# The end of a two-layer transformer kernel laid out anew: value products first, reciprocals on query rows, and one queue for last block, partials and leftovers

## The chip, the cores and the metric

The kernel runs on one core of a Trainium2 chip. Its engines work side by side, each through its own queue in order: TensorE (PE) multiplies matrices into the accumulation memory PSUM, VectorE (DVE) and ScalarE (ACT) do elementwise work, GpSimd (POOL) a few small things, SyncE (SP) issues transfers. The metric is device time in microseconds (us), the median of several runs; a profiled execution of the same program gives the trace that is read here.

## The reference

Two kinds of layer alternate over 2048 rows of 512 numbers. Softmax attention with 32 query heads of width 16 shares one key and one value head; a feed-forward layer of width 1792 uses ReLU. Each has a layer norm ahead of it and a residual around it.

```python
def _A_ref(x, wq, wk, wv, wo):
    q = (x @ wq).reshape(B, S, H, Dh).transpose(0, 2, 1, 3)
    k = x @ wk
    v = x @ wv
    p = softmax(einsum("bhqd,bkd->bhqk", q, k) * Dh ** -0.5)
    o = einsum("bhqk,bkd->bhqd", p, v)
    return o.transpose(0, 2, 1, 3).reshape(B, S, H * Dh) @ wo

def _B_ref(x, w1, w2):
    return relu(x @ w1) @ w2

x = x + _A_ref(_layernorm(x), A_wq, A_wk, A_wv, A_wo)
x = x + _B_ref(_layernorm(x), B_w1, B_w2)
x = x + _A_ref(_layernorm(x), A_wq, A_wk, A_wv, A_wo)
x = x + _B_ref(_layernorm(x), B_w1, B_w2)
```

## The kernel before

The program is fully unrolled. A plain and slower version of it (`exact`, tag x) stands behind a check of the inputs' range and does not run here; all names in the trace begin with f, the fast version's tag.

**Units and steps.** The rows are cut into four blocks of 512 queries. A unit U is four heads of one block, so each layer has 32 units, and each unit has 16 steps, one for each 128 keys. A step is two score products into the PSUM tiles st0 and st1 (each 128 x 2 x 512 numbers, two banks of 2 KB a partition), an exponential on ACT for each into the tile p, and a value product on PE into the pair acc and acc2. The value rows carry a column of ones, so that the accumulators hold the unnormalised outputs and the softmax's sums side by side. Score and value products use 64x32 pieces of the array, 8 matmuls for a pass of 512 columns. A step can be *cut*: DVE splits p into two halves of 16 bits, and the value product takes 24 short matmuls instead of 8 in f32.

**Chains.** When a block's attention is done, a generator `chain(L, b)` issues all the rest of it in pieces, each a `yield`: the output projection with wo (row tiles s = 0 to 3 of 128 rows), the residual's *gain* (`added`, a DVE operation that reads PSUM and adds to xt), the norm's statistics (`stats`: two DVE operations, then two on POOL) and its `apply`, the transposition back into xt, then for pairs of 128 hidden columns `up` (ReLU on ACT into hh, the low part hl on DVE, both reading PSUM) and, for four of them at a time, `down` with a second gain. In f16 each product is three matmuls, high by high, high by low and low by high.

**The planner.** `timed` lays out the steps by a model of the engines' clocks (`_Account`): whenever PE is free it looks ahead over three choices, a score, a value product or a piece of leftover work from the chains, and takes the first move of the best sequence. What it chooses is PE's order for good. While steps run, leftover work goes through 64x32 pieces in two PSUM tiles named misc (`batch`), with a small read by DVE (`seen`) between its two turns. When no steps are left the kernel is *solo*: a job is then twelve (or six) full 128x128 matmuls, `mm3`, into the next of two misc tiles, read by ACT and DVE. A chain's generator says "lag" when its next piece isn't ready by the planner's account.

**The end, `closing`.** The last two units, 62 and 63, do not go through memory as the others do but stay on the chip (`ends`). The old order is: the 9 *partials* of row tile 0 (the output projection's three finished quarters, `out_early`), `joined`, the other 27 partials, the first weights of the last block (`fetch`), then a loop that gives PE to the last block's chain whenever the planner's account says it is ready, and else to the leftovers of the block before. `joined` multiplies each end with two matrices of zeros and ones (`make_joins`), in f32: one picks the outputs, one spreads each head's sum over its 16 rows. DVE takes 512 reciprocals a partition of the spread sums, then multiplies, and ACT and DVE split the rows into high (ot2[0]) and low (ot2[1]). Three *finals* for each row tile complete the output projection. The partials and finals of row tiles 0 and 1 are accumulated in the two halves of st0, those of 2 and 3 in the two halves of st1. The last chain transposes its normed rows through acc and acc2 and goes on to `up` and `down` in solo form. `bounded`, `least` and `flag` check ranges, between its first pieces.

The planner's account compares exact regions of a tile. The order of PE against the readers of PSUM on the chip is made by the compiler's framework, from the program's order and the tiles that are read and written.

Of the kernel before, what the change touches and what calls it, by code (L numbers as in the profile page):

```python
# [9 lines left out]
F32 = mybir.dt.float32  # L10
# [4 lines left out]
AF = mybir.ActivationFunctionType  # L15
ALU = mybir.AluOpType
AX = mybir.AxisListType.X
MAX, MUL, SUB, ADD = ALU.max, ALU.mult, ALU.subtract, ALU.add

P = 128  # L20
S = 2048
D = 512
# [202 lines left out]
class _Net:  # L225
# [54 lines left out]

    def misc(self):
        return self.pp.tile([P, D], F32, name=self.tag + "misc", bufs=3 if self.exact else 2)
# [721 lines left out]
    def out_early(self, s):  # L1004

        if s % 2 == 0:
            self.bank = self.pp.tile([P, 2, D], F32, name=f"{self.tag}st{s // 2}")
        ps = self.bank[:, s % 2]
        ops = [o for G in range(3) for o in self.out_parts(s, G)]
        for i, (a, b) in enumerate(ops):  # L1010
            self.nc.tensor.matmul(ps, a, b, start=(i == 0), stop=False)
        self.early = (self.early or []) + [ps]

    def joined(self):

        nc, V = self.nc, self.nc.vector
        l, o = (self.pp.tile([P, D], F32, name=self.tag + n) for n in ("acc", "acc2"))
        for k, ps in ((1, l), (0, o)):
            for u in range(2):
                nc.tensor.matmul(ps, self.joins[:, k, u], self.ends[u], start=(u == 0), stop=(u == 1))  # L1020
        r = self.ends_inverse = self.wt("rinv", [P, D])
        t = self.wt("oraw", [P, D])
        h, low = self.ot2[0][:, 3], self.ot2[1][:, 3]
        for c in (slice(0, 256), slice(256, D)):
            V.reciprocal(r[:, c], l[:, c])
            V.tensor_mul(t[:, c], o[:, c], r[:, c])
            nc.scalar.activation(h[:, c], t[:, c], AF.Copy)
            V.tensor_sub(low[:, c], t[:, c], h[:, c])

    def bounded(self):  # L1030

        r, t = self.ends_inverse, self.wt("oraw", [P, D])
        m = self.wt("kmx", [P, 4], bufs=1)
        self.nc.vector.tensor_scalar(t, r, 1.0 / LMAX, None, op0=ALU.is_ge)
        self.nc.vector.scalar_tensor_tensor(t, r, 1.0 / LMIN, t, op0=ALU.is_le, op1=MUL)
        self.nc.vector.tensor_reduce(m[:, 0:1], t, axis=AX, op=ALU.min)
        self.nc.vector.tensor_mul(self.good[:, 0:1], self.good[:, 0:1], m[:, 0:1])

    def make_joins(self):

        self.joins = self.wq2[0].bitcast(F32).rearrange("p c (u m) -> p (c u) m", u=2)[:, 0:4].rearrange(
            "p (k u) m -> p k u m", k=2)
        self.nc.gpsimd.memset(self.joins.rearrange("p k u m -> p (k u m)"), 0.0)
        v = self.ident.rearrange("p (j t d) -> p j t d", t=2, d=DH)
        for u in range(2):
            for k, src in enumerate((v[:, :, 0], v[:, :, 1, 0:1].to_broadcast([P, 4, DH]))):
                dst = self.joins[:, k, u, 64 * u:64 * u + 64].rearrange("p (j d) -> p j d", d=DH)
                self.nc.gpsimd.tensor_copy(dst, src)

    def closing(self, chain):  # L1050

        self.out_early(0)
        self.joined()
        for s in range(1, 4):
            self.out_early(s)
        self.fetch(1, NB - 1)
        old, self.gens = self.gens, []
        chain()
        main, free, outs = self.gens, 0.0, self.outs
        while old:  # L1060
            turn = main if self.outs == outs and self.now >= free else old
            self.gens, self.solo = turn, turn is main
            w = self.advance()
            if turn is main:
                free = self.free if isinstance(w, tuple) else 0.0
        self.gens, self.solo = main, True
# [3 lines left out]
    def chain(self, L, b):  # L1070
# [38 lines left out]
        if self.early:  # L1109
            for s in range(4):  # L1110
                ps, parts = self.early[s], self.out_parts(s, 3)
                yield from self.soon([x for o in parts for x in o])
                for i, (x, y) in enumerate(parts):
                    nc.tensor.matmul(ps, x, y, start=False, stop=(i == 2))
                    yield 1.0
                added(s, ps)
                todo.append(self.stats(xs[s]))
                ready(s)
                if s:
                    todo[s - 1] = self.apply(*todo[s - 1])  # L1120
                if s > 1:
                    yield from self.transposed(todo[s - 2], s - 2, bank="acc2" if s > 2 else "acc")
            todo[3] = self.apply(*todo[3])
            for s in (2, 3):
                yield from self.transposed(todo[s], s, bank="acc2" if s > 2 else "acc")
# [411 lines left out]
    def timed(self, steps, operands, ready, front, back, product, after, cut):  # L1537
# [66 lines left out]
        while len(done) < n:  # L1604
            k, j, due = state[5:8]
            cut_some()
            if chance and self.now >= chance[0][0] - LATE:
                e1, e, i = chance.pop()
                if (self.asked and self.gens and due >= 3.0 and not pend and i > j and self.coming > NEAR
# [18 lines left out]
            kind = choose(state)  # L1628
            rate = self.rate(step, due) if self.gens else 0.0
# [272 lines left out]
```

## Time and profile before

| what | value |
|---|---|
| runs shown | 2226.67 us median of 3 (2226.18 to 2227.86) |
| profiled execution, its own time | 2224.62 us |
| its span from first to last instruction | 2222.7 us, mean clock of PE 0.994 |
| last exponential issued | 2105.40 us from the span's start |
| first up-projection of the last block | 2142.68 us |
| last output transfers issued from | 2212.57 us |

All times inside the trace count from the start of the span. A row of the timeline gives start, duration, engine, operation, output and input tile, shape, count, and in brackets how long the engine was idle before it and what released it. All instructions show line L193, the helper through which the planner records them, so the tile names tell them apart: p and acc are the steps, fmisc leftovers and solo jobs, fst scores and the last output projection, ot the attention rows, xt residual rows and transposed rows. Rows with "| busy, mean ns | idle" are groups. Rows that begin with a stretch of time give for each of PE, PEld (weight loads), DVE, ACT and POOL the busy time and count, then the granted clock of PE (1.00 is full), the share of transfers and GB/s. A matmul's shown end includes its way through the array, so in a run of full-size matmuls the starts lie 0.2157 us apart while each lasts 0.38.

### The profile page before, as it was taken

To read this page: it belongs to the slowest core of one execution; us is meant where nothing else is said; L and a number is where in the kernel's file an instruction comes from. 1 tells how busy PE (TensorE), PEld (TensorE's weight loads), DVE (VectorE), ACT (ScalarE), POOL (GpSimd) and SP (SyncE) were. 2 spreads that over 40 slices of the span, in tenths; PEclk is the share of its full clock that TensorE was granted. 3 is DMA by queue.
4 is the path that set the end of the run, shared out by engine and by line. 5 is a ranking of instruction groups with operands and counts; after the bars stand their busy time and mean duration, and the time that the engine had idled before them with its cause. 6 is when DMAs were issued, how large, how long until landed. Compare 5 with 4: busy or idle time off the path is not lost.

```text
span 2222.7 us, 127244 instructions
## 1 busy us (share of the span) xinstructions
PE 2147.8 (97%) x59873; PEld 1255.0 (56%) x59873; DVE 1207.4 (54%) x1944; ACT 1980.6 (89%) x2112; POOL 280.3 (13%) x320
## 2 busy tenths in 40 slices
PE   7999999999999999999999999999999999999988
PEld 3444446665667555555546855557555556565533
DVE  6526535544565555655575666565635545544552
ACT  6999999999889999999988889989999999999810
POOL 6317720001100021000120021100000000100000
PEclk8999999999999999999999999999999999999999
DMA  6335633212332133221242154422123211412122
GB/s 155 85 115 188 196 92 100 68 42 60 79 100 68 46 99 72 87 67 41 84 120 75 40 138 146 155 84 68 40 74 119 65 53 65 98 48 77 47 82 73
DMA packets 182801, 195.08 MB, mean 88 GB/s; under 512 B 79560, under 2 KB 115960, under 8 KB 182008
## 3 DMA queue, kind: packets, MB, share of 16 engines
q1 hardware_dynamic: 182264, 186.83, 28.6%
q8 instruction: 470, 7.70, 1.4%
q14 instruction: 67, 0.55, 0.1%
HBM read 120.16 MB, written 51.87 MB: 77 GB/s over the span
## 4 chain that ended last, share of the span: by engine, by line
PE 77%; ACT 17%; DVE 3%; issue 2%; DMA 1%; POOL 1%; SPq 0%; ACTq 0%; DVEq 0%; POOLq 0%
PE fmisc L193 30%; PE facc L193 30%; ACT fp L193 16%; PE fst L193 16%; DVE fxt L193 0%; DVE fbst L193 0%; DVE faccs L193 0%; DVE fp L193 0%; DVE fkop L193 0%; DMA fw<-fwd 0%; POOL fxp L193 0%; POOL fbmv L193 0%; DVE fkv L193 0%; DMA fxr<-fxt 0%; DVE fxn L193 0%
## 5 line engine op out<-in xcount | busy, mean ns | idle before, releaser
L193 ACT ACTIVATE fp<-fst 128x1024 f32<-128x1024 f32 x2048 | 1948.6, 1031 | 124.3 <-PE fst L193 110.4
L193 PE MATMUL fst<-fqop,fkop 64*32 64x512 f16 x16384 | 936.2, 378 | 45.4 <-ACT fp L193 36.2
L193 PE MATMUL facc<-fp,fva 64*32 64x512 f32 x13520 | 933.3, 591 | 1.8 <-DVE faccs L193 1.2
L193 PEld LDWEIGHTS <-fkop 64*32 64x32 f16 x16384 | 379.6, 91 | 476.6 <-issue 368.1
L193 DVE TENSOR_TENSOR fp<-fp 128x1024 f16<-128x1024 f32 x358 | 481.5, 1397 | 255.5 <-ACT fp L193 255.4
L193 PEld LDWEIGHTS facc<-fp,fva 64*32 64x32 f32 x13520 | 295.9, 106 | 90.4 <-issue 20.4
L193 PE MATMUL fmisc<-fw,fhh 64*32 64x512 f16 (+1 forms) x6384 | 310.8, 377 | 6.1 <-DVE fxt L193 3.2
L193 PEld LDWEIGHTS <-fw 64*32 64x32 f16 (+1 forms) x9576 | 208.9, 93 | 119.9 <-issue 35.4
L193 PE MATMUL fmisc<-fxt,fw 64*32 64x512 f16 (+1 forms) x5544 | 236.0, 376 | 3.1 <-issue 1.6
L193 POOL TENSOR_SCALAR fbmv<-fbmv 128x1 f32<-128x1 f32 x64 | 18.8, 294 | 1555.0 <-DVE fbmv L193 1554.1
L193 PE MATMUL fmisc<-fw,fhl 64*32 64x512 f16 (+1 forms) x3192 | 196.5, 378 | 0.0
L193 PEld LDWEIGHTS <-fhh 64*32 64x32 f16 (+1 forms) x6384 | 135.7, 93 | 93.4 <-issue 42.4
L193 DVE SCALAR_TENSOR_TENSOR fxt<-fmisc,fxt 128x512 f32<-128x512 f32 x156 | 102.5, 683 | 146.9 <-PE fmisc L193 146.7
L193 PE MATMUL facc<-fp,fvp 64*16 64x512 bf16 (+2 forms) x4296 | 167.2, 386 | 0.0
L193 PE MATMUL fmisc<-fxq,fw 64*32 64x512 f16 x4032 | 153.1, 376 | 0.9 <-issue 0.3
L193 DVE COPY fseen<-fmisc 1x1 f32<-1x1 f32 x266 | 28.6, 141 | 188.1 <-PE fmisc L193 187.8
L193 DVE TENSOR_SCALAR fhh<-fmisc 128x512 f16<-128x512 f32 x98 | 67.2, 686 | 113.8 <-PE fmisc L193 113.7
L193 DVE TENSOR_TENSOR faccs<-faccs,facc 128x512 f32<-128x512 f32 x116 | 79.7, 687 | 68.6 <-PE facc L193 56.5
L193 PEld LDWEIGHTS <-fvp 64*32 64x32 f16 (+1 forms) x4296 | 84.4, 90 | 41.0 <-issue 10.9
L193 PE MATMUL fmisc<-fwo,fot 64*32 64x512 f16 x2688 | 103.0, 379 | 3.2 <-issue 3.2
L193 DVE SCALAR_TENSOR_TENSOR fhl<-fmisc,fhh 128x512 f16<-128x512 f32 x112 | 77.5, 692 | 28.4 <-ACT fhh L193 25.0
L193 PEld LDWEIGHTS <-fhl 64*32 64x32 f16 (+1 forms) x3192 | 68.2, 93 | 32.6 <-issue 4.6
(148 smaller groups left out, 1102.8 us busy)
## 6 DMA issues: line engine op xcount, KB each, us to landing
fw<-fwd SPq DMA_DIRECT2D x224, 256.0 KB
fod<-faccs SPq DMA_DIRECT2D x62, 256.0 KB
fqop<-fqd SPq DMA_DIRECT2D x152, 98.0 KB
fxt<-in_A_x_dram SPq DMA_DIRECT2D x32, 256.0 KB
fqd<-fqh SPq DMA_DIRECT2D x64, 128.0 KB
foraw<-fod SPq DMA_DIRECT2D x31, 256.0 KB
frinv<-frd SPq DMA_DIRECT2D x31, 256.0 KB
faccs<-in_B_w_dram SPq DMA_DIRECT2D x28, 256.0 KB
```

Source lines behind the costliest of these rows:

```text
L193: r = fn(*a, **k)
```

## The change

In the steps: no step of the last two may be cut any more, and when all scores are issued a value product goes ahead of leftovers.

In `joined`, now a generator inside the last chain: eight small products of the ends with four columns of the identity give the sums on query rows (128 queries a partition, 32 numbers); DVE takes the reciprocals of these and copies them 16 wide; four transpositions bring them back to head rows, where they multiply the joined outputs, which one pair of f32 products still makes.

In `closing`: the partials become a list. One loop issues the last chain's piece if it is ready, else a leftover if that is ready, else a partial; once the last block's output projection is done, leftovers come ahead of it. The chain issues the partials of a row tile that are still missing just ahead of its finals, and the norms' `apply` and the transpositions follow after all four row tiles.

In `misc`: once `closing` has begun, the solo chain's jobs take the four halves of st0 and st1 in turn (`ring`) in place of the two misc tiles.

```diff
     def misc(self):
+        if self.ring and self.solo:
+            self.ring = self.ring[1:] + self.ring[:1]
+            return self.ring[-1]
         return self.pp.tile([P, D], F32, name=self.tag + "misc", bufs=3 if self.exact else 2)
...
-    def out_early(self, s):
-
-        if s % 2 == 0:
-            self.bank = self.pp.tile([P, 2, D], F32, name=f"{self.tag}st{s // 2}")
-        ps = self.bank[:, s % 2]
-        ops = [o for G in range(3) for o in self.out_parts(s, G)]
-        for i, (a, b) in enumerate(ops):
-            self.nc.tensor.matmul(ps, a, b, start=(i == 0), stop=False)
-        self.early = (self.early or []) + [ps]
+    def out_early(self):
+
+        self.early = []
+        for s in range(4):
+            if s % 2 == 0:
+                bank = self.pp.tile([P, 2, D], F32, name=f"{self.tag}st{s // 2}")
+            self.early.append(bank[:, s % 2])
+        self.partial = [(s, k, o) for s in range(4) for k, o in enumerate(
+            [o for G in range(3) for o in self.out_parts(s, G)])]
+
+    def out_next(self):
+
+        s, k, (a, b) = self.partial.pop(0)
+        self.nc.tensor.matmul(self.early[s], a, b, start=(k == 0), stop=False)
 
     def joined(self):
...
+        for u in range(2):
+            yield from self.soon([self.ends[u]], [l, o])
+            for t in range(4):
+                nc.tensor.matmul(v[:, t, u], self.ends[u][:, t * P:(t + 1) * P], ones, start=True, stop=True,
+                                 skip_group_check=True)
+            yield 1.0
+        r = self.ends_inverse = self.wt("lsum", [P, 2, 32])
+        V.reciprocal(r[:, 0], l[:, 0:32])
+        wide = self.wt("rinv", [P, 4, 8, DH])
+        V.tensor_copy(wide, r[:, 0].rearrange("p (t h) -> p t h", t=4)[:, :, :, None].to_broadcast([P, 4, 8, DH]))
+        for u in range(2):
+            nc.tensor.matmul(o, self.joins[:, u], self.ends[u], start=(u == 0), stop=(u == 1))
+            yield 4.0
+        t0 = self.wt("oraw", [P, D])
+        nc.scalar.activation(t0, o, AF.Copy)
+        back = self.pp.tile([P, D], F32, name=self.tag + "acc")
+        yield from self.soon([wide], [back])
+        for t in range(4):
+            nc.tensor.transpose(back[:, t * P:(t + 1) * P], wide[:, t].rearrange("p h d -> p (h d)"), self.ident)
+        yield 1.0
         h, low = self.ot2[0][:, 3], self.ot2[1][:, 3]
         for c in (slice(0, 256), slice(256, D)):
-            V.reciprocal(r[:, c], l[:, c])
-            V.tensor_mul(t[:, c], o[:, c], r[:, c])
-            nc.scalar.activation(h[:, c], t[:, c], AF.Copy)
-            V.tensor_sub(low[:, c], t[:, c], h[:, c])
+            V.tensor_mul(t0[:, c], t0[:, c], back[:, c])
+            nc.scalar.activation(h[:, c], t0[:, c], AF.Copy)
+        for c in (slice(0, 256), slice(256, D)):
+            V.tensor_sub(low[:, c], t0[:, c], h[:, c])
...
     def closing(self, chain):
 
-        self.out_early(0)
-        self.joined()
-        for s in range(1, 4):
-            self.out_early(s)
+        self.out_early()
+        self.ring = self.early
         self.fetch(1, NB - 1)
         old, self.gens = self.gens, []
         chain()
-        main, free, outs = self.gens, 0.0, self.outs
-        while old:
-            turn = main if self.outs == outs and self.now >= free else old
-            self.gens, self.solo = turn, turn is main
+        main, outs = self.gens, self.outs
+        free = {False: self.free, True: 0.0}
+        while old or self.outs == outs:
+            late = self.outs > outs
+            first = free[True] <= self.now
+            if old and free[False] <= self.now and (late or not first):
+                turn = False
+            elif not first and self.partial:
+                self.out_next()
+                continue
+            else:
+                turn = first or not old or free[True] <= free[False]
+            self.gens, self.solo = (main if turn else old), turn
+            self.sim.at["PE"] = max(self.now, free[turn])
             w = self.advance()
-            if turn is main:
-                free = self.free if isinstance(w, tuple) else 0.0
+            free[turn] = self.free if isinstance(w, tuple) else 0.0
...
         if self.early:
+            yield from self.joined()
             for s in range(4):
+                while self.partial and self.partial[0][0] <= s:
+                    self.out_next()
+                    yield 1.0
                 ps, parts = self.early[s], self.out_parts(s, 3)
...
-                if s > 1:
-                    yield from self.transposed(todo[s - 2], s - 2, bank="acc2" if s > 2 else "acc")
-            todo[3] = self.apply(*todo[3])
-            for s in (2, 3):
-                yield from self.transposed(todo[s], s, bank="acc2" if s > 2 else "acc")
+            for s in range(4):
+                yield from self.transposed(todo[s], s, bank="acc2" if s % 2 else "acc")
+                if s == 0:
+                    todo[3] = self.apply(*todo[3])
...
-                if (self.asked and self.gens and due >= 3.0 and not pend and i > j and self.coming > NEAR
+                if (self.asked and self.gens and due >= 3.0 and not pend and j < i < n - 2 and self.coming > NEAR
...
             kind = choose(state)
+            if k == 2 * n and state[8] and state[8][0] <= self.now + DENSE:
+                kind = "product"
```

`make_joins` fills half as much and copies two matrices instead of four; `bounded` checks the reciprocals on query rows, 32 numbers a partition instead of 512.

More of the change, by code (lines that the diff above doesn't have):

```diff
@@ L279, in raw @@
         return self.wt("wraw", shape, bufs=4) if self.exact else self.wt("accs", shape, bufs=5)
+    ring = None
     def misc(self):
+        if self.ring and self.solo:
+            self.ring = self.ring[1:] + self.ring[:1]
+            return self.ring[-1]
         return self.pp.tile([P, D], F32, name=self.tag + "misc", bufs=3 if self.exact else 2)
@@ L1014, in joined @@
+    def out_next(self):
+        s, k, (a, b) = self.partial.pop(0)
+        self.nc.tensor.matmul(self.early[s], a, b, start=(k == 0), stop=False)
     def joined(self):
         nc, V = self.nc, self.nc.vector
[L1017 to L1021, printed above, removed]
@@ L1022, in joined @@
-        t = self.wt("oraw", [P, D])
+        o, l = (self.pp.tile([P, D], F32, name=self.tag + n) for n in ("acc2", "acc"))
+        ones = self.ident.rearrange("p (j x) -> p j x", x=32)[:, :, DH]
+        v = l[:, 0:32].rearrange("p (t u j) -> p t u j", t=4, u=2)
+        for u in range(2):
[4 more added lines that the diff above has]
+            yield 1.0
@@ L1030, in bounded @@
+        for c in (slice(0, 256), slice(256, D)):
+            V.tensor_sub(low[:, c], t0[:, c], h[:, c])
     def bounded(self):
-        r, t = self.ends_inverse, self.wt("oraw", [P, D])
+        r = self.ends_inverse
         m = self.wt("kmx", [P, 4], bufs=1)
-        self.nc.vector.tensor_scalar(t, r, 1.0 / LMAX, None, op0=ALU.is_ge)
-        self.nc.vector.scalar_tensor_tensor(t, r, 1.0 / LMIN, t, op0=ALU.is_le, op1=MUL)
-        self.nc.vector.tensor_reduce(m[:, 0:1], t, axis=AX, op=ALU.min)
+        self.nc.vector.tensor_scalar(r[:, 1], r[:, 0], 1.0 / LMAX, None, op0=ALU.is_ge)
@@ L1037, in bounded @@
+        self.nc.vector.scalar_tensor_tensor(r[:, 1], r[:, 0], 1.0 / LMIN, r[:, 1], op0=ALU.is_le, op1=MUL)
+        self.nc.vector.tensor_reduce(m[:, 0:1], r[:, 1], axis=AX, op=ALU.min)
         self.nc.vector.tensor_mul(self.good[:, 0:1], self.good[:, 0:1], m[:, 0:1])
     def make_joins(self):
-        self.joins = self.wq2[0].bitcast(F32).rearrange("p c (u m) -> p (c u) m", u=2)[:, 0:4].rearrange(
-            "p (k u) m -> p k u m", k=2)
-        self.nc.gpsimd.memset(self.joins.rearrange("p k u m -> p (k u m)"), 0.0)
+        self.joins = self.wq2[0].bitcast(F32).rearrange("p c (u m) -> p (c u) m", u=2)[:, 0:2]
@@ L1044, in make_joins @@
+        self.nc.gpsimd.memset(self.joins.rearrange("p u m -> p (u m)"), 0.0)
         v = self.ident.rearrange("p (j t d) -> p j t d", t=2, d=DH)
         for u in range(2):
-            for k, src in enumerate((v[:, :, 0], v[:, :, 1, 0:1].to_broadcast([P, 4, DH]))):
-                dst = self.joins[:, k, u, 64 * u:64 * u + 64].rearrange("p (j d) -> p j d", d=DH)
-                self.nc.gpsimd.tensor_copy(dst, src)
+            dst = self.joins[:, u, 64 * u:64 * u + 64].rearrange("p (j d) -> p j d", d=DH)
+            self.nc.gpsimd.tensor_copy(dst, v[:, :, 0])
```

## Prediction

> **What bounds the kernel now.** I read the page's busy times first, then the chain of waits, then a table of the last 117 us by stage, then the timeline of those stages.
>
> ```profile
> PE 2147.8 (97%) x59873; PEld 1255.0 (56%) x59873; DVE 1207.4 (54%) x1944; ACT 1980.6 (89%) x2112; POOL 280.3 (13%) x320
> 2106.00:2123.20 17.20, 17.20 (x207) 7.75 (x199) 7.13 (x10) 1.86 (x4) 0.00 (x0) 1.00 0.01 1
> 2123.20:2142.70 19.50, 12.16 (x219) 5.75 (x218) 12.85 (x28) 2.28 (x4) 3.59 (x8) 0.91 0.25 82
> 2142.70:2215.80 73.10, 73.00 (x339) 32.84 (x339) 23.19 (x41) 8.36 (x14) 0.00 (x0) 1.00 0.27 88
> 2215.80:2222.70 6.90, 0.00 (x0) 0.00 (x0) 0.62 (x1) 0.00 (x0) 0.00 (x0) 0.76 0.23 83
> ```
>
> PE is the bound nearly everywhere. The change touches only what lies behind the last scores at about 2106, so the table holds all that can move: a stage where PE is full, the seam of 19.50 us where it works 12.16 (7.3 us idle), 73.1 us of the last block's matrices with PE full, and a tail of output transfers that nothing here alters. The PEclk column (0.91) says that the seam also lost clock. Its pieces:
>
> ```profile
> 2108.67 1.05 PE L193 MATMUL facc<-fp,fva 64*32 64x512 f32 x16
> 2109.53 0.89 PE L193 MATMUL facc<-fp,fvp 64*32 64x512 bf16 x24
> 2110.21 1.06 PE L193 MATMUL facc<-fp,fva 64*32 64x512 f32 x16
> 2111.20 2.12 PE L193 MATMUL fst<-fwo,fot 128*128 128x512 f16 x9
> 2113.16 3.60 PE L193 MATMUL facc<-faccs,fwqh 128*128 128x512 f32 x8
> 2115.07 1.76 DVE L193 RECIPROCAL frinv<-facc 128x256 f32<-128x256 f32 x1 [2.37 <-PE facc L193]
> 2116.59 6.64 PE L193 MATMUL fst<-fwo,fot 128*128 128x512 f16 x30
> 2120.88 0.43 DVE L193 TENSOR_TENSOR fot<-foraw,fot 128x256 f16<-128x256 f32 x1 [0.48 <-ACT fot L193]
> 2123.26 0.69 DVE L193 SCALAR_TENSOR_TENSOR fxt<-fst,fxt 128x512 f32<-128x512 f32 x1 [1.96 <-PE fst L193]
> 2124.01 1.45 PE L193 MATMUL fst<-fwo,fot 128*128 128x512 f16 x6 [0.78 <-DVE fxt L193]
> 2124.85 0.69 DVE L193 SCALAR_TENSOR_TENSOR fxt<-fst,fxt 128x512 f32<-128x512 f32 x1
> 2129.07 0.41 PE L193 MATMUL fmisc<-fw,fhh 64*32 64x512 f16 x8 [2.19 <-DVE fseen L193]
> 2129.41 0.66 PE L193 MATMUL facc<-fident,fxn 128*128 128x128 f32 x4
> 2135.32 0.40 PE L193 MATMUL fmisc<-fw,fhh 64*32 64x512 f16 x4 [2.96 <-DVE fxt L193]
> 2142.68 8.79 PE L193 MATMUL fmisc<-fxt,fw 128*128 128x512 f16 x40 [0.92 <-DMA fw<-fwd]
> 2137.25:2140.90 3.65, 3.36 (x65) 1.36 (x72) 1.50 (x4) 0.77 (x2) 0.00 (x0) 0.53 0.99 307
> ```
>
> The last values run until 2111; the joining product and slow reciprocals finish the attention rows at 2121.3 (the fot row of DVE at 2120.88). Then PE waits in turn for gains, norms and the leftover's evacuations until the block's first up-projection at 2142.68.
>
> One row decides this prediction: at 2124.01 PE waited 0.78 us for DVE. The 30 matmuls at 2116.59 are 27 partials and the three finals of row tile 0. The six at 2124.01 are the finals of row tiles 1 and 2. Their data were complete at 2121.3, yet they start 0.06 us after the gain of tile 0 ends (2123.26 + 0.69). Tile 0 sits in the first half of st0, tile 1 in the second. Row tile 2, in st1, did not wait for the gain of tile 1, which began only at 2124.85. So writing one half of an st tile is held back by a reader of its other half. The change leans on these halves everywhere.
>
> **The change, part by part.** I count PE time in units of one 512-column fp16 pass.
>
> ```profile
> 2168.91 10.52 PE L193 MATMUL fmisc<-fxt,fw 128*128 128x512 f16 x48
> 2171.70 0.60 ACT L193 ACTIVATE fhh<-fmisc 128x512 f16<-128x512 f32 x1 [12.35 <-PE fmisc L193]
> 2172.33 0.69 DVE L193 SCALAR_TENSOR_TENSOR fhl<-fmisc,fhh 128x512 f16<-128x512 f32 x1 [2.53 <-ACT fhh L193]
> 2182.06 0.69 DVE L193 SCALAR_TENSOR_TENSOR fxt<-fmisc,fxt 128x512 f32<-128x512 f32 x1 [1.27 <-PE fmisc L193]
> L193 ACT ACTIVATE fhh<-fmisc 128x512 f16<-128x512 f32 x14 | 8.4, 597 | 54.4 <-PE fmisc L193 54.4
> L193 PE MATMUL fst<-fwo,fot 128*128 128x512 f16 x48 | 11.0, 379 | 0.8 <-DVE fxt L193 0.8
> L193 PE MATMUL fmisc<-fw,fhh 64*32 64x512 f16 x128 | 6.7, 443 | 5.6 <-DVE fxt L193 3.2 <-DVE fseen L193 2.5
> L193 PE MATMUL fmisc<-fw,fhl 64*32 64x512 f16 x64 | 3.9, 461 | 0.0
> L193 PE MATMUL facc<-fident,fxn 128*128 128x128 f32 x16 | 2.4, 279 | 0.0
> ```
>
> One unit is (10.52 - 0.38) / 47 = 0.2157 us.
>
> *Values first.* In the old order 96 leftover matmuls (12 units, 2.6 us) stand between 2106.08 and the last three value products. With the new rule they come after. No value step n-2 is halved now: 0.86 us (2108.67 to 2109.53) for 0.68 (2109.53 to 2110.21), +0.2. Last value at 2106.0 + 3 x 0.86 = 2108.6 instead of 2111. The leftover is not saved, only moved; all of it (12 + 192/8 = 36 units, 7.8 us) now lies in the weave.
>
> *Joining.* Removed: two of four f32 products (3.45 us of starts to 1.72) and two reciprocals of 1.76 on DVE. Added on PE: eight products with 128x128 f32 weights and four columns, two passes each by the joining row (8 records for 4 products). No such shape is in the trace. The nearest is the f32 transpose, which loads the same weights: four in 0.66, about 0.12 us apart, so 16 x 0.12 = 1.9. Bounds: one pass each, 1.0; a pass like the joining one per 0.19 us weight load, 3.0. I take 1.8, and 0.6 for four transposes more. DVE gets a 32-column reciprocal (0.35) and a widening copy (0.42 to 0.69), both under the joining product that PE runs meanwhile. ACT's copy of that product is 0.60.
>
> ```profile
> L193 DVE RECIPROCAL flsum<-flsum 128x32 f32<-128x32 f32 x31 | 10.9, 353 | 1.1
> L193 DVE TENSOR_SCALAR foraw<-frinv 128x512 f32<-128x512 f32 x1 | 0.4, 417 | 0.0
> L193 PEld LDWEIGHTS facc<-faccs,fwqh 128*128 128x128 f32 x8 | 1.5, 190 | 1.6 <-issue 1.2 <-PE facc L193 0.2
> ```
>
> By hand: sums in rows at 2112.5, product at 2114.2, transposes to 2114.9, then four half-width steps in a row (multiply, ACT copy, ACT copy, subtract) of some 0.45 with their gaps, as the fot row's 0.43: rows complete at 2116.9, against 2121.3.
>
> *The weave.*
>
> ```profile
> 2111.38 0.60 ACT L193 ACTIVATE faccs<-facc 128x512 f32<-128x512 f32 x1 [4.95 <-PE facc L193]
> 2112.01 0.69 DVE L193 TENSOR_TENSOR faccs<-faccs,facc 128x512 f32<-128x512 f32 x1 [1.79 <-ACT faccs L193]
> L193 DVE BATCH_NORM_STATS2 fbst<-fxt 128x6 f32<-128x512 f32 x4 | 2.8, 695 | 0.1
> L193 DVE TENSOR_SCALAR fxn<-fxt,fbmv 128x512 f32<-128x512 f32 x4 | 2.1, 523 | 0.1
> L193 DVE TENSOR_TENSOR fxt<-facc,fxt 128x512 f16<-128x512 f32 x4 | 2.7, 687 | 3.4 <-ACT fxt L193 3.4
> ```
>
> The last block goes first whenever it can, leftovers fill its waits, partials the rest. Following its rules: nine leftover units while the accumulators are copied and added (0.60 + 0.69 and their hops, to 2110.5), then the chain above; nine partials of row tile 0, two leftover units, three finals; then tiles 1, 2, 3 with nine partials and three finals each, without a planned wait. But tiles 1 and 3 share a tile of PSUM with 0 and 2, whose gain has just been issued, so each starts 0.95 us late (0.78 shown, plus 0.17 from a matmul's last issue to its shown end): 1.9 us. The finals of tile 3 end near 2127.8. DVE then has gain, statistics, two applies (one behind POOL), four subtractions of about 0.7 and the leftover's two gains between them, about 7 us. PE meanwhile has the transposes, one leftover unit and six more; I count stalls of 1.5, 0.45 and 0.85. The remaining 18 leftover units mix with the first up-projection.
>
> PE's ledger from 2106.0, in us: values 2.6, leftovers 7.8, partials and finals 48 units or 10.4, sums 1.8, product 1.7, transposes 0.6 + 2.4, together 27.3. Before it was 26.4. Thirteen changes between 64x32 and full-size tiles at 0.12 (values end their issue at 2111.07, the next matmul starts 2111.20): 1.6. Waits 1.9 + 2.8. So the up-projection stands as if begun at 2106.0 + 33.6 = 2139.6, against 2142.7: 3.1 us gained. Bounds: 0.5 (sums at 3.0, and the 1.7 us that half clock from 2137.25 to 2140.90 cost before, over again) to 5.5 (sums at 1.0 and half of the stalls gone).
>
> *SP, POOL, the check.* The up-projection's loads of weights are issued before, no longer behind, the leftover's outputs; nothing waits. The joins' fill is one memset half as long and two copies fewer, on a POOL 13% busy. The bounds check shrinks from 512 to 32 columns on DVE, which is off the path in the last stage (23.19 of 73.10 us). Each is counted at zero; PE's work covers them.
>
> *The ring of four halves.* The diff's first hunk costs most. Once the ring is set, the last block's up- and down-projections no longer take turns in two separate misc tiles but run through st0's two halves, then st1's. There are 14 up jobs (14 fhh rows) and 16 down jobs, always in pairs, so every second job writes the half beside the one just filled and must wait until that was read. An up job issued from 2168.91 takes 12 units, to 2171.50; ACT and then DVE read it until 2173.02; PE could resume at 2173.07: 1.57 us lost. A down job has only the gain: the next job's issue at 2181.86, gain over at 2182.75, resume at 2182.81: 0.95 lost. Seven pairs of up, eight of down: 7 x 1.57 + 8 x 0.95 = 18.6 us. Today all of it is hidden by the second misc tile (73.00 of 73.10 busy); nothing else stands ready, as PE issues in order and the leftover is used up. Bounds: 17 (the first pair's wait filled by leftovers) to 20 (DVE late on some).
>
> **Sum.** -3.1 + 18.6 = +15.5 us. The profiled execution took 2224.62 us, 2.0 under the median of 2226.67; it would be 2240.1, and the median 2242.2.
>
> **A rule against this.** The Trainium skill, PSUM — Partial Sum Buffer, section "PSUM bank collisions raise a hardware error", says that TensorE and VectorE must be kept apart only per bank and 32-partition quadrant, and that accesses to different banks run clean. By that rule two 2 KB halves need no wait, and the sum would be the first rival's. The row at 2124.01 disagrees with it as a description of this program: the wait is there.
>
> **Rivals.** *Halves are independent after all.* Then neither the ring nor tiles 1 and 3 wait: -3.1 - 1.9 = -5.0 us, 2221.7, faster. For it: nothing else in the trace shows a wait between halves, and one wait of 0.78 us is thin. Against: the operands were ready and tile 2 went through unheld. It decides in one place: whether the second up job starts when the first ends.
>
> *Only unfinished sums are held.* The finals at 2124.01 continue an accumulation; the ring's jobs start new ones. If that makes the difference, 3.1 us remain gained: 2223.6, within the noise.
>
> *The clock gives way too.* Before, the clock fell only after a stretch as thin as this:
>
> ```profile
> 2130.40:2133.80 3.40, 1.96 (x46) 1.02 (x45) 2.99 (x6) 0.90 (x2) 0.66 (x2) 1.00 0.00 0
> 2133.80:2137.20 3.40, 1.68 (x16) 1.05 (x15) 1.95 (x4) 0.26 (x1) 0.28 (x1) 1.00 0.32 118
> ```
>
> The ring's pairs keep PE busier (5.2 of 6.7 us), so I expect full clock. If each up pair brought a fall like the 3.65 us at 0.53, it would cost 7 x 1.7 = 12 us more: 2254. The Trainium skill, TensorE: Matmul & The Clock Gate, section "A second HAM failure mode: psum-queue depth-cycling", describes such a fall from short pauses between groups; no run here shows it so far.
>
> **How the numbers follow.** Forecast 0.85, independent halves 0.06, only unfinished sums 0.04, clock 0.05. About 0.2% (4.5 us) is what a measurement can tell from no change. The forecast and the clock case are slower, 0.90; the second rival is the same, 0.04; the first is faster, 0.06. The range takes the ends of both sizes, -5.5 + 17 to -0.5 + 20, or 2238 to 2246, and a little for a weave other than I followed: 2236 to 2247.
>
> **What would show it.** Last value product near 2108.6; fot complete near 2117; the up-projection's writes now named fst; in the last stage PE idle about 1.4 us before seven of its groups, released by DVE fhl, and 0.8 before eight, released by DVE fxt; that stage some 91 us. If PE there is full, I am wrong about the halves. If the waits are there but shorter, DVE reads sooner than I count; if the first stage gains nothing, the weave stalls on DVE.

## The result: 0.9% slower, 21 us, by the mechanism forecast

The changed kernel took 2247.72 us, the median of four runs (2244.92 to 2254.91). The kernel before took 2226.43 us on the same chip (2225.66 to 2227.86). The ratio is 1.0094, with a 95% interval of 1.0076 to 1.0113. Forecast were 2242.2 us and a range of 2236 to 2247. The profiled execution of the changed kernel took 2245.25 us, its span 2243.4 us. Two more measurements of the same kernel, further down, put the loss at 15.2 and 14.2 us.

I read the change in the order in which the work runs. First comes the profile page's line of busy times of the changed kernel, and then its first three stages, with the columns of before's table.

```profile
PE 2154.0 (96%) x59881; PEld 1249.5 (56%) x59881; DVE 1202.5 (54%) x1943; ACT 1981.7 (88%) x2112; POOL 279.2 (12%) x318
```

```profile
2106.00:2123.20 17.20, 16.42 (x284) 8.63 (x262) 5.47 (x13) 4.79 (x7) 0.58 (x2) 1.00 0.15 48
2123.20:2147.40 24.20, 19.68 (x275) 9.36 (x273) 13.86 (x28) 2.88 (x5) 3.00 (x7) 0.93 0.08 29
2147.40:2236.90 89.50, 74.35 (x327) 32.04 (x326) 20.85 (x39) 7.76 (x13) 0.00 (x0) 0.98 0.22 73
```

The page's shares hardly moved (PE 97% before, 96% now); the stages show it. The last stage has changed its kind. PE was busy 73.00 of 73.10 us there before; now it is busy 74.35 of 89.50, so 15.1 us of idleness are new. (The work is the same but for the first job, which now lies ahead of the stage.) The chain that ended last, in order of time (start, duration, what; steps under 0.1 us are left out), shows the pattern that repeats through this stage:

```profile
2175.33 5.35 PE fst L193 x24
2180.75 0.60 ACT fhh L193
2181.38 0.70 DVE fhl L193
2182.13 5.35 PE fst L193 x24
2187.56 0.61 ACT fhh L193
2188.20 0.70 DVE fhl L193
```

Each run of 24 is two jobs of 12 units: one in the second half of one st tile, then one in the first half of the other. The job after it wants the second half of that other tile. PE stands until ACT and DVE have read the first half, and the next run starts some 0.05 us after DVE ends. ACT and DVE, hidden before, now lie on the chain once for each pair. The view of waits gives the totals of the changed kernel from 2104 to 2240 (who waited for whom: us, times, longest):

```profile
PE fst L193 <- DVE fhl L193: 10.9, 7, 2.0
PE fst L193 <- DVE fxt L193: 7.8, 10, 0.8
PE facc L193 <- DVE fxt L193: 1.7, 2, 1.1
```

Seven waits on fhl, and eight plus two on fxt: the counts forecast. The rows ahead of that stage, from the timeline of the changed kernel:

```profile
2052.38 0.58 SPq L193 DMA_DIRECT2D foraw<-fod  x1
2109.55 2.76 PE L193 MATMUL facc<-fp,fva 64*32 64x512 f32 x48
2113.97 1.95 PE L193 MATMUL facc<-fident,faccs 128*128 128x4 f32 x16
2115.78 1.96 PE L193 MATMUL facc<-faccs,fwqh 128*128 128x512 f32 x4
2117.58 0.60 PE L193 MATMUL facc<-fident,frinv 128*128 128x128 f32 x4
2118.02 2.75 PE L193 MATMUL fst<-fwo,fot 128*128 128x512 f16 x12
2119.31 0.76 DVE L193 TENSOR_TENSOR fot<-foraw,fot 128x256 f16<-128x256 f32 x2
2121.55 5.34 PE L193 MATMUL fst<-fwo,fot 128*128 128x512 f16 x24 [0.78 <-DVE fxt L193]
2127.67 2.75 PE L193 MATMUL fst<-fwo,fot 128*128 128x512 f16 x12 [0.78 <-DVE fxt L193]
2147.40 7.03 PE L193 MATMUL fst<-fxt,fw 128*128 128x512 f16 x24 [2.01 <-DVE fhl L193]
2162.86 2.32 PE L193 MATMUL fst<-fxt,fw 128*128 128x512 f16 x10 [1.57 <-DVE fhl L193]
2236.89 0.69 DVE L193 SCALAR_TENSOR_TENSOR fxt<-fst,fxt 128x512 f32<-128x512 f32 x1 [1.55 <-PE fst L193]
```

**A yardstick.** The first of these rows is the last transfer of attention rows back onto the chip. The program up to the last steps is the same in both kernels, yet this transfer was issued at 2049.54 us in before's trace and at 2052.38 here. Those 2.8 us are drift of identical work. So I compare traces by the time from this transfer to the start of the last gain, and call it the touched stretch. In before these rows are:

```profile
2049.54 0.58 SPq L193 DMA_DIRECT2D foraw<-fod  x1
2215.73 0.69 DVE L193 SCALAR_TENSOR_TENSOR fxt<-fmisc,fxt 128x512 f32<-128x512 f32 x1 [0.60 <-PE fmisc L193]
```

The touched stretch was 166.19 us before and is 184.51 us now, 18.3 more. This adds up: 2224.62 + 18.3 + 2.8 of drift - 0.5 (the tail behind the last gain is 0.5 us shorter) = 2245.2, and the profiled execution took 2245.25.

The yardstick is not perfect. Between the transfer and the last cut value product, in all traces still the same steps, identical code took from 51.1 to 52.0 us. So a difference of less than about 1 us between two single traces shows little.

### The profile page after: what moved, and what is told of

Read it like the earlier page. It is cut to its first block, busy times and chain, and to the rows that moved or that the text cites. A ratio compares the mean times of both kernels' runs of the same rounds, so it can differ in the third digit from the quotient of the medians.

```text
span 2243.4 us, 127261 instructions
## 1 busy us (share of the span) xinstructions
PE 2154.0 (96%) x59881; PEld 1249.5 (56%) x59881; DVE 1202.5 (54%) x1943; ACT 1981.7 (88%) x2112; POOL 279.2 (12%) x318
## 4 chain that ended last, share of the span: by engine, by line
PE 77%; ACT 15%; DVE 4%; issue 2%; DMA 1%; POOL 1%; SPq 0%; ACTq 0%; DVEq 0%; POOLq 0%
PE facc L193 30%; PE fmisc L193 27%; PE fst L193 19%; ACT fp L193 15%; DVE fxt L193 1%; DVE faccs L193 0%; DVE fbst L193 0%; DVE fp L193 0%; DMA frd<-flsum 0%; DVE fkop L193 0%; DMA fqop<-fqd 0%; DVE fhl L193 0%; DMA fqd<-fqh 0%; SPq L193 0%; POOL fxp L193 0%
## 5 line engine op out<-in xcount | busy, mean ns | idle before, releaser
L193 PE MATMUL fst<-fqop,fkop 64*32 64x512 f16 x16384 | 949.6, 378 | 44.8 <-ACT fp L193 36.1
L193 PEld LDWEIGHTS <-fkop 64*32 64x32 f16 x16384 | 384.4, 91 | 476.2 <-issue 364.3
L193 PE MATMUL fmisc<-fw,fhh 64*32 64x512 f16 x6272 | 279.4, 377 | 0.5 <-DVE fseen L193 0.3
L193 PE MATMUL fmisc<-fxt,fw 64*32 64x512 f16 x5376 | 202.6, 376 | 4.3 <-issue 3.6
L193 PE MATMUL fmisc<-fw,fhl 64*32 64x512 f16 x3136 | 178.2, 377 | 0.0
L193 PE MATMUL facc<-fp,fvp 64*32 64x512 bf16 (+2 forms) x4272 | 169.0, 387 | 0.0
L193 DVE SCALAR_TENSOR_TENSOR fxt<-fmisc,fxt 128x512 f32<-128x512 f32 x140 | 91.4, 682 | 121.0 <-PE fmisc L193 120.8
L193 PEld LDWEIGHTS <-fot 64*32 64x32 f16 (+1 forms) x2736 | 57.5, 93 | 41.9 <-issue 17.2
```

The costliest lines, as they stand in the source:

```text
L193: r = fn(*a, **k)
```

## The experiments

*Theory:* a write to one half of an st tile is held until readers of the other half are done, so the ring makes pairs wait. *Rivals:* the waits come from something else that the weave does (DVE late, the clock); or only unfinished sums are held. After the first measurement the runs were made in three groups, each with its own runs of before on the same chip. A *half-clock fall* is a stretch of about 3.5 us in which the granted clock stands near 0.5; the last column counts those inside the touched stretch.

| kernel | median us (runs) | before | ratio, 95% interval | touched stretch us | half-clock falls |
|---|---|---|---|---|---|
| before, profile | | | | 166.2 | 1 |
| after | 2247.72 (4) | 2226.43 | 1.0094 (1.0076 to 1.0113) | 184.5 | 2 |
| a_again | 2242.86 (6) | 2227.71 | 1.0071 (1.0054 to 1.0088) | 183.1 | 1 |
| e_before_ring | 2242.84 (4) | 2227.71 | 1.0074 (1.0059 to 1.0088) | 183.7 | 2 |
| e_ring_order | 2225.09 (10) | 2227.71 | 0.9994 (0.9983 to 1.0005) | 163.1 | 1 |
| e_alternate | 2223.05 (12) | 2227.71 | 0.9980 (0.9969 to 0.9991) | 160.2 | 0 |
| a_third | 2243.25 (5) | 2229.02 | 1.0065 (1.0051 to 1.0079) | 182.9 | 1 |
| e_alt_free | 2224.21 (8) | 2229.02 | 0.9977 (0.9967 to 0.9988) | 160.1 | 0 |
| e_alt_no_first | 2222.40 (8) | 2229.02 | 0.9977 (0.9967 to 0.9987) | 158.9 | 0 |
| e_alt_old_join | 2218.23 (4) | 2229.02 | 0.9952 (0.9937 to 0.9967) | 159.2 | 0 |
| e_weave_only | 2223.63 (12) | 2227.45 | 0.9980 (0.9969 to 0.9991) | 160.5 | 1 |
| e_before_alt | 2229.05 (10) | 2227.45 | 1.0007 (0.9994 to 1.0020) | 165.2 | 2 |

**a_again, the changed kernel once more, no edit.**

> The changed kernel once more, nothing edited, for two questions: how far its times scatter, and whether the profiled run is again some 2.8 us behind the kernel before already at 2050 us, where both programs are still the same. If that drift is chance, the new profile shows another one (anywhere from -2 to +4 us) and the median lies near 2245; if it belongs to this program, the profile shows 2.8 us again and the median lies near 2248. In both cases PE waits 7 times for DVE fhl (some 11 us) and 10 times for DVE fxt (some 8 us) ahead of writes to fst.

It took 15.2 us more than before, 6 us less than the first measurement said, and its touched stretch is 1.4 us shorter. The view of waits reads 10.9 and 7.8 again, so the waits are fixed. What differs is the clock and the runs' scatter (2239.12 to 2250.28). The two signs of the expectation disagree: the transfer came 2.9 us behind before's again (2052.44), but the median fell below 2245. a_third, further down, decides it.

**e_before_ring, the kernel before with the ring alone.**

```diff
+        if self.ring and self.solo:
+            self.ring = self.ring[1:] + self.ring[:1]
+            return self.ring[-1]
...
         for s in range(1, 4):
             self.out_early(s)
+        self.ring = self.early
```

> The kernel before, with nothing but the ring: its solo jobs of the last block go through the halves of st0 and st1 in the changed kernel's order in place of the two misc tiles. Theory: the ring alone costs 7 x 1.57 + 8 x 0.95 = 18.6 us: 2244 to 2246. Rival (weave): 2226, since nothing of the weave is in it.

The ring alone costs 15.1 us by the medians, and 17.5 us in the touched stretch; the median lies 1 us under the range expected. Its waits:

```profile
PE fst L193 <- DVE fhl L193: 10.0, 7, 1.5
PE fst L193 <- DVE fxt L193: 7.0, 9, 0.8
```

Seven and nine (one of the nine is the wait that before had at 2124.01): the weave, the joining and the new order of values have no part in them. By the rule for the shown waits (10.0 + 8 x 0.78 + 15 x 0.165) the pairs cost 18.7. The touched stretch shows 1 us less, since the last block's first up-projection starts 92.1 us behind the yardstick's transfer, where before took 93.1 with 0.92 us on a transfer of weights (timeline of e_before_ring):

```profile
2135.59 0.40 PE L193 MATMUL fmisc<-fw,fhh 64*32 64x512 f16 x4 [1.41 <-DVE fxt L193]
2142.11 2.76 PE L193 MATMUL fst<-fxt,fw 128*128 128x512 f16 x12
2146.28 4.04 PE L193 MATMUL fst<-fxt,fw 128*128 128x512 f16 x18 [1.41 <-DVE fhl L193]
```

The first row is the likely reason why its additional half-clock fall, from 2130, is not seen in the sum: the wait for DVE that followed was 1.41 us, where before had 2.96.

**e_ring_order, the changed kernel with the same four halves in another order.** The change is one line. Nothing else differs, neither the memory nor the jobs:

```diff
-        self.ring = self.early
+        self.ring = [self.early[i] for i in (0, 2, 1, 3)]
```

> The changed kernel with only the ring's order changed, to first half of st0, first half of st1, second half of st0, second half of st1; partials and finals as changed. Theory: the 15 waits of the ring go (10.9 + 6.2 us as shown, 19.6 with the ways through the array), the two of row tiles 1 and 3 stay at 0.78 each: median 2226 to 2228, 2 us over the alternating one. Rival (weave): above 2238.

Now two successive jobs never lie in one tile. The waits on fhl are gone, and of those on fxt the two of the finals remain, as the view of waits of e_ring_order shows, and its last stage is full:

```profile
PE facc L193 <- DVE fxt L193: 1.7, 2, 1.1
PE fst L193 <- DVE fxt L193: 1.6, 2, 0.8
```

```profile
2147.30:2215.00 67.70, 67.70 (x316) 30.53 (x314) 20.84 (x38) 7.76 (x13) 0.00 (x0) 1.00 0.27 90
```

The touched stretch fell from 183.1 and 182.9 (the two traces with one half-clock fall, as here) to 163.1, so the pairs cost 19.8 to 20.0 us. By the medians it is 17.8 (2242.86 to 2225.09, which lies 1 us under the range expected). This is the run that tells the theory from its rivals: the jobs start new sums, so it is not unfinished sums that are held, and the weave on DVE is the same.

**e_alternate, the row tiles alternate between st0 and st1 too.**

```diff
-            if s % 2 == 0:
-                bank = self.pp.tile([P, 2, D], F32, name=f"{self.tag}st{s // 2}")
-            self.early.append(bank[:, s % 2])
+        banks = [self.pp.tile([P, 2, D], F32, name=f"{self.tag}st{i}") for i in range(2)]
+        self.early = [banks[s % 2][:, s // 2] for s in range(4)]
```

> The changed kernel with the row tiles 0 to 3 (and with them the ring) laid on st0, st1, st0, st1 by turns, so that no two neighbours share a tile; the planner's order is the same to the last instruction. Theory (a write to one half waits for the readers of the other half): all 17 waits of PE go, 10.9 + 7.8 us as shown and about 0.165 each for the way through the array, 21.5 us: profiled execution 2224 and median 2224 to 2226, the same as the kernel before or 1 to 3 us faster. Rival (the new weave itself is slower, by late leftovers and lost clock): the time stays above 2238.

The profiled execution took 2224.20 us as expected, and the median, 2223.05, lies 1 us under the range. The 48 products of the last output projection now run without a break, where the changed kernel had 12, 24 and 12 with 0.78 us between (timeline of e_alternate, then its waits, then two stages):

```profile
2120.69 10.52 PE L193 MATMUL fst<-fwo,fot 128*128 128x512 f16 x48
```

```profile
PE facc L193 <- DVE fxt L193: 1.7, 2, 1.1
PE fmisc L193 <- DVE fxt L193: 0.2, 1, 0.2
```

```profile
2123.20:2144.99 21.79, 19.87 (x282) 8.95 (x280) 13.52 (x28) 2.88 (x5) 3.57 (x8) 1.00 0.07 26
2144.99:2215.00 70.01, 70.01 (x334) 31.72 (x327) 22.72 (x41) 7.76 (x13) 0.00 (x0) 1.00 0.28 91
```

No wait on a neighbour half is left. The kernel is 0.2% faster than before, 4.7 us by the medians and 6.0 in the touched stretch. About 1.7 of the 6.0 may be before's half-clock fall, which this trace doesn't have.

**a_third, the changed kernel a third time, no edit.**

> The changed kernel a third time, nothing edited. The identical part of both programs ended between 0.5 and 5.7 us later at 2050 us than in the first profile of before, by chance, so the time is expected to scatter again: median 2241 to 2249. The stretch that the change touches, from the last transfer into foraw to the start of the last gain of DVE, was 166.2 us in the kernel before and 184.5 and 183.1 in two profiles of the changed one; if the excess over the forecast of +15.5 lies in that stretch it is 183 to 185 again, if it is chance of the rest it comes nearer 181.7.

14.2 us over before, with the same waits. The touched stretch, 182.9 us, lies with the 183 of a_again and not near 181.7. The transfer came at 2055.68 us, 6.1 behind before's, so the 2.8 and 2.9 seen earlier do not belong to the program. Over all 15 runs the changed kernel's median is 2243.8 us.

**e_alt_free, e_alternate with the transpositions of tiles 2 and 3 in halves that are free already,** so that they need not wait for DVE to read acc and acc2.

```diff
+                ps = self.early[s - 2] if bank == "early" else ...
...
+                yield from self.transposed(todo[s], s, bank="early" if s > 1 else ...)
```

> The alternating kernel, with the transpositions of row tiles 2 and 3 in halves of st0 and st1 whose gains are long done, in place of waiting for acc2 and acc to be read. If these two waits of PE (1.12 and 0.60 us) lie on the path, the touched stretch shrinks from 160.2 to some 158.5 us and the median to 2221. If DVE's queue of subtractions and gains sets the start of the up-projection, the waits only move and it stays at 160 to 161.

It ended like e_alternate (160.1 against 160.2). The waits of e_alt_free from the same stretch tell why:

```profile
PE fst L193 <- DVE fxn L193: 1.1, 2, 0.6
PE fmisc L193 <- DVE fxt L193: 0.7, 2, 0.5
```

The 1.7 us on DVE's reading of acc became 1.8 us on other operations of DVE. So it was not the accumulator that PE waited for in the end: what DVE still had to do set the start there.

**e_alt_no_first, e_alternate with the planner's two edits undone.**

```diff
-                if (... and j < i < n - 2 and self.coming > NEAR
+                if (... and i > j and self.coming > NEAR
...
-            if k == 2 * n and state[8] and state[8][0] <= self.now + DENSE:
-                kind = "product"
```

> The alternating kernel without the two edits of the planner in the steps (cuts near the end allowed again, no value product ahead of leftovers). By the path (values end 2.6 us later, so everything does) the touched stretch grows from 160.2 to 162.5 or so, median 2225 to 2226. By PE's ledger (the same work in another order, with fewer leftovers and two gains fewer in DVE's queue at the end) it stays within 1 us of 160.2.

Values first brings nothing that can be seen: without it the touched stretch is 1.3 us shorter, and the medians (2222.40 here, 0.9977; 0.9980 for e_alternate) cannot tell the two apart. These are the last cut value product and the last exponential, in e_alternate and then in e_alt_no_first:

```profile
2107.00 0.88 PE L193 MATMUL facc<-fp,fvp 64*32 64x512 bf16 x24
2112.48 1.02 ACT L193 ACTIVATE fp<-fst 128x1024 f32<-128x1024 f32 x1 [1.39 <-PE fst L193]
```

```profile
2104.19 0.88 PE L193 MATMUL facc<-fp,fvp 64*32 64x512 bf16 x24
2108.59 1.03 ACT L193 ACTIVATE fp<-fst 128x1024 f32<-128x1024 f32 x1 [0.32 <-PE fst L193]
```

Counted from the first row of each, up to which the steps are the same, the difference is only 0.6 us (108.5 against 107.9 to the last gain); the rest of the 1.3 is drift. With the edits the last exponential comes 5.5 us behind that row, without them 4.4: PE issues the last score behind a value product and a leftover, and ACT waits 1.39 us for it in place of 0.32. So the edits act before the scores end, too, and not only behind them, as the prediction had it.

**e_alt_old_join, e_alternate with `joined`, `make_joins` and `bounded` as before** (as a generator in the same place: long reciprocals on DVE, four f32 products).

```diff
+        for k, ps in ((1, l), (0, o)):
+            for u in range(2):
+                yield from self.soon([self.ends[u]], [ps])
+                nc.tensor.matmul(ps, self.joins[:, k, u], self.ends[u], start=(u == 0), stop=(u == 1))
+                yield 4.0
...
+            V.reciprocal(r[:, c], l[:, c])
```

> The alternating kernel with the old joining (two f32 products for the spread sums, 512 reciprocals a partition, old check of them) inside the new weave. By the path (attention rows complete 4 us later: 3.5 us of reciprocals against 0.8) the touched stretch grows from 160.2 to 163 or 164, less what leftovers and partials fill. By PE's ledger (3.45 us of products against 1.7 + 1.8 + 0.6, and partials to fill the wait) it falls by 0.7 to 159.5.

The old joining is no worse: 159.2 against 160.2, and the fastest median of all, 2218.23. The four runs are few; its trace is only 1 us better than e_alternate's, the rest of that lead is not shown, and e_weave_only, which has the old joining too, does not repeat it.

**e_weave_only, both undone together:** alternating halves and the weave stay, values and joining as before.

> The alternating kernel with both parts taken out that seemed to cost about 1 us each: no edits of the planner in the steps, and the old joining. What is left of the change is the weave in the closing loop and the alternating halves. If the two parts are independent, the touched stretch is 160.2 - 1.3 - 1.0 = 158 us, median some 9 us under the kernel before (2218 to 2220). If they cost the same microsecond (both load PE just ahead of the seam), it stays at 159.

The expectation of the median, 2218 to 2220, failed: it is 2223.63, with the ratio of e_alternate, 0.9980. The touched stretch is 160.5, with one half-clock fall; less 1.7 us for it, an estimate, that is 158.8, much like each alone. That fits two parts that cost the same microsecond, but one trace of each, with drift of the same size, does not show it. What these runs show is that neither part brings a gain that can be told.

**e_before_alt, the kernel before with alternating halves and the ring, but without the weave.**

> The kernel before with alternating halves and the ring through them, no weave. If the gain of the alternating kernels comes from the weave, little is left: the wait of 0.78 us at the second row tile goes and the first up-projection need not wait for the leftovers' evacuation (0.92 us), so the touched stretch falls from 166.2 to some 164.5 us. If the alternation of halves is the gain, it falls to 160 or 161.

1.0007, no change that can be told, with the touched stretch at 165.2, near the 164.5 expected if the gain is the weave's. Against e_weave_only, in the same group, 4.8 us of touched stretch and 5.4 us of median are missing. PE's waits behind 2104 us say where, in e_before_alt and then in e_weave_only:

```profile
PE fmisc L193 <- DVE fseen L193: 3.1, 2, 2.8
PE fmisc L193 <- DVE fxt L193: 1.9, 2, 1.7
```

```profile
PE facc L193 <- DVE fxt L193: 1.5, 1, 1.5
PE facc L193 <- DVE fseen L193: 0.6, 1, 0.6
```

The weave took 2.9 us of these waits away, and e_before_alt has one half-clock fall more, about 1.7 us. So the weave is the part that gains; whether the additional fall belongs to the kernel without it or to chance, one trace doesn't tell.

## Why the mechanism was right, and which terms of the sum failed

**The halves: right.** The one wait of 0.78 us in before's trace carried the forecast, and it held. The ring alone accounts for the loss (e_before_ring), and the order of the same halves takes it away (e_ring_order). That the halves are independent and that only unfinished sums are held are both excluded for this program. PE can write one bank while DVE reads another: in the last stage of e_alternate it does so job after job, and PE is busy 70.01 of 70.01 us. That fits the Trainium skill, PSUM — Partial Sum Buffer, section "PSUM bank collisions raise a hardware error", which lets accesses to different banks run side by side. There the two banks belong to different tiles, though; no run here lets PE write one half of a tile while the other is read. The traces put each of the waits down to a signal from DVE, so what holds PE is most likely the order that the compiler's framework makes by whole tiles. That step is argued: a run that gives the two halves out as two tiles would show it, and if PE waited there too, it would be the neighbouring banks.

**The seam: the sum fits, in part by luck.** Forecast was a gain of 3.1 us apart from the ring. e_ring_order, which has all of the seam and none of the ring's waits, stands at 163.1 against 166.2: 3.1 (one trace each; the medians, at 0.9994, don't show it). Its steps, in the changed kernel's times less the drift of 2.8: the sums in rows took 1.81 us of starts (2113.97 to 2115.78; 1.8 forecast), the rows were complete at 2120.07 - 2.8 = 2117.3 (2116.9), tiles 1 and 3 waited 0.78 each. Two things were off, and they offset each other in part. The stalls on DVE were 1.1 and 0.6 us where I had 1.5, 0.45 and 0.85, so 1.1 us less. And the ledger has no half-clock fall, but e_ring_order has one in the seam, about 1.7 us. The last value product was late as well: its issue ended at 2112.13 - 2.8 = 2109.3, not 2108.6. The planner had put a score and leftovers between the last exponentials otherwise than I followed, and eight leftover units, not nine, came behind the values, so that little of it reached the rows. The independent halves were forecast at -5.0; e_alternate, which makes them so and has no fall, has -6.0. By their own terms the ends of the seam's range come to 0.2 and 5.3 us, not 0.5 and 5.5; nothing hangs on it.

**The ring: mis-sized by 1 us.** Forecast were 7 x 1.57 + 8 x 0.95 = 18.6. The waits shown are 10.9 for seven up pairs and 7.8 - 2 x 0.78 = 6.2 for the down pairs; with the 0.165 us of each of 15 from the last issue to its shown end that is 19.6, and e_ring_order says 19.8 to 20.0. I had taken 1.40 shown for each up pair. The first waited 2.01, as DVE was behind with the leftover's gains; the third waited 1.57, behind the range checks; four waited 1.46 or 1.47. The forecast bound of 20 named just that, "DVE late on some", but the central value left it out.

**The clock: at nothing in the sum, and it costs.** The ledger of the seam holds no half-clock fall; only the low end of its range holds one. For the ring's pairs I expected full clock. The changed kernel fell once or twice. The rows are the stretch ahead of each fall and the fall itself, in the changed kernel (PEclk is the column third from the end):

```profile
2131.10:2134.50 3.40, 1.68 (x31) 0.73 (x29) 3.21 (x8) 1.48 (x3) 0.94 (x2) 1.00 0.02 5
2134.40:2137.90 3.50, 3.45 (x52) 2.27 (x52) 2.48 (x4) 0.67 (x2) 0.00 (x0) 0.52 0.00 0
2144.80:2148.00 3.20, 1.19 (x27) 0.47 (x12) 1.89 (x3) 0.00 (x0) 0.00 (x0) 1.00 0.32 120
2148.00:2151.50 3.50, 3.50 (x10) 1.30 (x9) 0.00 (x0) 0.00 (x0) 0.00 (x0) 0.52 0.65 193
```

The second came with the first up pair's wait of 2.01 us. Each halves the clock for about 3.5 us and so costs up to 1.7, where no wait behind it gives way. But the rival in which every up pair brings a fall is wrong: the fall at 2148.00 alone takes 3.5 x 0.48 / 89.5 = 0.02 off the clock of the last stage, which stands at 0.98, so nothing fell behind it. My rule that the clock falls "only after a stretch as thin as this" was no good measure either: other cuts through before's trace find 0.44 us of PE work in 2132.3 to 2135.7, ahead of its fall, but also 1.21 in 2125.9 to 2129.3, with none behind it.

**The sum, and the steps that failed.** e_ring_order's 163.1 and the 19.6 of the ring's waits make 182.7, and a_again and a_third show 183.1 and 182.9; a second fall of 1.7 makes 184.4, and the first trace shows 184.5. My sum gave 166.2 + 15.5 = 181.7. The first profiled execution was to take 2240.1 us and took 2245.25. Of these 5.1 us, 1.0 is the ring, which I took too small (18.6 for 19.6), 1.7 is the second fall, which the sum puts at nothing, and about 2.3 is drift of the identical code ahead of the change, 2.8 less 0.5 in the tail, which the sum puts at nothing too. The first measurement's 2247.72 lies 0.7 us above my upper end of 2247 because the range was built of the same terms: "the ends of both sizes ... and a little for a weave". It had none for how much identical kernels scatter. Three runs of before within 1.7 us of each other had suggested that there is little. Later runs of before went from 2222.3 to 2232.9, and the changed kernel's from 2239 to 2255. Its three medians, 2247.7, 2242.9 and 2243.3, spread by almost 5 us for one and the same program; that 2242.2 is near two of them and near the 2243.8 of all runs is luck to that extent. Why two of the first four runs lay above 2250 isn't known: they left no trace.

**Chances.** The cases held 0.85 for the forecast, and its mechanism came. I gave the clock's rival 0.05 for a fall with each pair; the likely form, one or two falls at the seam, I should have put into the forecast itself.

## What to carry to other kernels

When buffers are given out in turn, look at which *allocation* each belongs to, not only at which memory: two successive jobs in halves of one tile were ordered here like two uses of one buffer, and the remedy was a permutation in one line. One unexplained wait of 0.8 us in a stage that is otherwise full is worth following, because it priced the whole change. Compare two traces from a common landmark ahead of the change, the latest that there is, and give a range at least the spread that identical programs show.

## What was not expected of the hardware

- Identical instructions (but for two copies on POOL) reach the same transfer between 2049.4 and 2057.0 us in these traces. The two ends, e_weave_only and then e_before_alt:

```profile
2049.43 0.58 SPq L193 DMA_DIRECT2D foraw<-fod  x1
2057.02 0.58 SPq L193 DMA_DIRECT2D foraw<-fod  x1
```

What sets this drift is open.

- PE need not be idle for its clock to fall: 1.68 busy of 3.40 us and 1.19 of 3.20 were followed by half clock for 3.5 us. The Trainium skill, TensorE: Matmul & The Clock Gate, section "What's actually happening", ties the fall to an idle window of about 3.4 us, and the return to as much sustained work. The length agrees; that the window be idle does not. Nor does a thin stretch always bring a fall. These are the seam's stretch in a_third, and the one ahead of the first up pair in a_again, both of the same program as the rows above; no fall followed either:

```profile
2134.40:2137.80 3.40, 1.68 (x30) 0.84 (x8) 3.25 (x8) 0.96 (x2) 0.94 (x2) 1.00 0.02 5
2144.60:2147.90 3.30, 1.29 (x49) 0.54 (x26) 1.89 (x3) 0.34 (x1) 0.00 (x0) 1.00 0.18 67
```

So how thin a stretch must be can't be read from these traces; what else decides is open.

- The ring's regular pauses, 1.4 us in each 6.8 with PE about 80% busy, left the clock at full speed in all three traces of the changed kernel, apart from the falls at the first up pair.
- Eight products with f32 weights of 128x128 and four columns take 16 passes in 1.95 us, 0.11 us each (1.81 / 16), close to the f32 transposes' 0.12.
